# RWKV scan feeding a gated MLP: a group's small matmul runs put side by side

## The chip, the cores and the metric

One core of a Trainium2 chip runs the whole program. The metric is the device time of one launch in microseconds; a kernel's figure is the median of several launches. TensorE (PE in the profile) does the matmuls and writes PSUM, which has eight banks of 512 float32 columns per partition. VectorE (DVE), ScalarE (ACT) and GpSimd (POOL) work beside it, and SyncE (SP) issues nearly all DMAs.

## What is computed

The reference is a linear recurrence over 768 steps for 4 batches and 8 heads of width 48, and then a gated MLP on its output, in float32:

```python
for t in range(S):
    cur = einsum('bhd,bhe->bhde', u * k[t], v[t])
    y[t] = einsum('bhd,bhde->bhe', r[t], state + cur)
    state = w * state + einsum('bhd,bhe->bhde', k[t], v[t])
...
x = y as (3072, 384)
out = (sigmoid(x @ w_gate) * (x @ w_val)) @ w_out     # 384 -> 1536 -> 384
```

## The kernel before

**Attention in groups.** The 768 steps are cut into 12 chunks of 64, and each chunk into two groups of 16 (batch, head) pairs: 24 groups, `n` = 0 to 23. A group needs four runs of 16 small matmuls, all in float32, so the trace counts two passes each and shows 32:

- `from_state` (L314): the decayed state times the queries, into two banks `yb[n]`. It is the first writer of y.
- `scores` (L329): keys times queries, into the two banks `sc`. `keep` (L345) then copies the masked scores to SBUF on VectorE.
- `apply` (L360): masked scores times values, added into the same y banks.
- `outer` (L379): keys times values, the new part of the state, into the upper columns of the y banks. `add_state` (L405) adds it to the state on VectorE, after `decay_state` (L396) on ScalarE.

`x_high` (ScalarE) and `x_low` (VectorE) then split y into two parts for the MLP; `fills` moves some rows of it by DMA. `prepare` makes the next group's inputs on GpSimd and VectorE (`bonus`, `queries`, `keys`, `token_keys`).

**MLP in items.** Two chunks make a tile of 512 columns; there are six tiles (`ti`), with 12 slices of the hidden width (`f`) each. An item is one tile and one slice: `up` (L465, 18 matmuls of 512 columns into two banks), the gate (`sigmoid` on ScalarE, `product` on VectorE, `h_high` on ScalarE, `h_low` on GpSimd), and one item later `down` (L504, 9 matmuls of 512 columns into three accumulators). Weights and activations are split in a high and a low part, which is why there are three passes of everything.

**PSUM.** Eight banks: two for `sc`, three that `one_bank` hands out in turn (`ring`: the two of `up`, and the two of y), three accumulators.

**What sets the order.** The order on all engines is the program's own; each engine works its queue in that order. The first two tiles' groups (0 to 7) and the first tile's items (0 to 13) run in an order written out by hand, the string `START`: there `U.12` is `up` of item 12, `D.11` `down` of item 11, `Z.8` `scores` of group 8, `K` `keep`, `Rv` `queries` on VectorE, `ov` the low part of a weight on VectorE, `A` and `T` `bonus` and `token_keys`. From item 14 on a loop runs: in the slices `SLOTS` (0, 3, 6, 9) of tiles 1 to 4 it takes a group along, for the tile after; that is a slot, and there are 16, groups 8 to 23. TensorE then works `up(i)`, `from_state`, `scores`, `down(i-1)`, `apply`, `outer`, `up(i+1)`. The last tile has items only.

**End of a tile.** `store` (L521) copies the three accumulators, half on ScalarE and half on VectorE, through buffers `wf`, of which the pool has two, and stores them. `store_last` does it for the last tile: accumulators 0 and 1 whole, the third in halves, one on each engine.

Of the kernel before, what the change touches and what calls it, by code (L numbers as in the profile page):

```python
# [19 lines left out]
P = 128  # L20
# [17 lines left out]
SLOTS = (0, 3, 6, 9)  # L38
# [12 lines left out]
W.11 j.9 m.9 I.7 d.7 D.8 ov.8 w.9 o.9 O.7 H.9 h.7 s.7 l.7 F.7 c.10 qv.9 U.10 D.9 g.10 j.10 k.8 w.10  # L51
m.10 U.11 H.10 F.6 c.11 ov.10 g.11 qv.10 D.10 j.11 U.12 m.11 H.11 g.12 qv.11 w.11 A.8 T.8 ov.11 m.12
Rv.8 H.12 D.11 q.12 U.13 g.13 D.12 m.13 H.13 q.13
# [4 lines left out]
def rwkv_then_moe(ctx: ExitStack, tc: tile.TileContext, wd, ch, tk, rt, ut, wt, rk0, vn0, wd0, out):  # L58
# [121 lines left out]
    def token_turn():  # L180
        for be in range(2):
            turn[be] = pacc.tile([P, 512], F32, name=f"acc{be}").rearrange("q (p x) -> q p x", x=64)
        for p in range(NP):
            for a in range(2):
                for be in range(2):
                    row = slice(64 * be, 64 * be + 64)
                    nc.tensor.matmul(
                        turn[be][64 * a : 64 * a + 64, p], pw[row, 2 * p + (a ^ be), 32:96],
                        masks[row, 1], start=True, stop=True,
                    )  # L190
# [58 lines left out]
    xt, dec, ga, yb = {}, {}, {}, {}  # L249
# [26 lines left out]
    def bonus(n):  # L276
        g = GROUPS[n][1]
        r, k = dec_of(n)[:, 1, 0 : 8 * D], toks[n][:, 0, 0 : 8 * D]
        nc.gpsimd.tensor_tensor(r, r, ub[:, g], ALU.mult)
        rows = r.rearrange("q (b p x) -> q b p x", b=2, p=2)  # L280
        nc.gpsimd.tensor_tensor(
            rows, rows, k.rearrange("q (p b x) -> q b p x", b=2, p=2), ALU.mult
        )
        nc.vector.tensor_reduce(
            gains[n % 2], r.rearrange("q (h d) -> q h d", d=D), axis=mybir.AxisListType.X, op=ALU.add
        )
# [73 lines left out]
    def apply(n):  # L360
        c, g = GROUPS[n]
        v, t = toks[n][:, 1], score[n % 2]
        if n < FIRST:
            yb[n] = one_bank(), one_bank()
            if c:
                from_state(n)
                nc.tensor.drain()
        for p, p2 in PP:
            for s in range(2):
                for gm in range(2):  # L370
                    be, row = gm ^ s, slice(64 * gm, 64 * gm + 64)
                    m, at = D if s else 64, (4 * p + 2 * be + p2) * D
                    i = (4 * be + 2 * p + p2) * C
# [5 lines left out]
    def outer(n):  # L379
        k, v = toks[n][:, 0], toks[n][:, 1]  # L380
        for p, p2 in PP:
            for be in range(2):
                for gm in range(2):
                    row, at = slice(64 * gm, 64 * gm + 64), (4 * p + 2 * be + p2) * D
                    m, o = D if be else 64, 256 + (2 * p + p2) * D
                    into_y(
                        n, be, gm ^ be, m, slice(o, o + D), k[row, at : at + m],
                        v[row, at : at + D], True,
                    )
# [15 lines left out]
    def add_state(n):  # L405
        g, st = states(n)
        for s in range(2):
            y = yb[n][s][0:112, 256 : 256 + 4 * D].rearrange("q (p x) -> q p x", p=2)
# [51 lines left out]
    class Moe:  # L460
        def __init__(self, x, acc, cols):
            self.x, self.acc, self.cols = x, acc, cols
            self.pair, self.sg, self.h = {}, {}, {}
# [34 lines left out]
        def gate(self, f):  # L498
# [3 lines left out]
            self.h_low(f)  # L502

        def down(self, f):  # L504

            h, w = self.h.pop(f), (whi[f], wlo[f])
            todo = [(k, d) for k in range(3) for d in range(3)]
            if f == NF - 1:
                todo.sort(key=lambda kd: kd[1])
            for k, d in todo:  # L510
                a, b = PASS[k]
                nc.tensor.matmul(  # L512
                    self.acc[d][:, self.cols], w[a][:, 2 * DM + d * P : 2 * DM + (d + 1) * P],
                    h[:, b, self.cols], start=(f == 0 and k == 0 and self.cols.start == 0),
# [16 lines left out]
    def store_last(acc, c):  # L531
        copies = nc.scalar.copy, nc.vector.tensor_copy
        for d in range(2):
            o = wtmp.tile([P, W3], F32, name="wf")[:, 0:512]
            copies[d](out=o, in_=acc[d])
            nc.sync.dma_start(
                out=out[d * P : (d + 1) * P, c : c + 2], in_=o.rearrange("q (c t) -> q c t", t=CT)
            )
        for i in range(2):
            o = hp.tile([P, 512], F32, name="sg")[:, 0:CT]  # L540
            copies[i](out=o, in_=acc[2][:, i * CT : (i + 1) * CT])  # L541
            nc.sync.dma_start(out=out[2 * P : 3 * P, c + i], in_=o)
# [9 lines left out]
    def moe_of(it):  # L552
# [3 lines left out]
        if (ti, h) not in moes:  # L556
            cols = (slice(0, CT), slice(CT, 2 * CT), slice(0, 2 * CT))[h]
            moes[ti, h] = Moe(xt[ti], accs[ti], cols)
        return moes[ti, h]

    def finish(i):
        ti, h, f = items[i]
        moe_of(items[i]).down(f)
        if f == NF - 1:
            if ti == len(TILES) - 1:
                store_last(accs[ti], TILES[ti][0])
# [6 lines left out]
        "tu": load_gains, "A": lambda n: bonus_keys(n) if n < FIRST else bonus(n), "R": queries,  # L573
# [22 lines left out]

    def prepare(n):
        if n < len(GROUPS):
            bonus(n)
            queries(n)  # L600
            keys(n)
            if GROUPS[n][0] < NC - 1:
                token_keys(n)

    def load(n):
        if n < len(GROUPS):
            load_channels(n)
            load_tokens(n)

    n = FIRST  # L610
    load(n + 1)

    for i in range(n0, len(items)):
# [3 lines left out]
        m.gate(f)  # L617
        attend = f in SLOTS and n < 4 * (ti + 2) and n < len(GROUPS)
        if attend:
            scores(n)  # L620
            if n + 1 < len(GROUPS):
                load_receptance(n + 1)
            if GROUPS[n][0] < NC - 1:
                decay_state(n)
            keep(n)
        finish(i - 1)
        if attend:
            apply(n)
            if GROUPS[n][0] < NC - 1:
                outer(n)  # L630
            x_high(n)
            x_low(n)
            if GROUPS[n][0] < NC - 1:
                add_state(n)
            prepare(n + 1)
            fills(n)
            load(n + 2)
            n += 1
# [193 lines left out]
```

## Time and profile before

| what | value |
|---|---|
| time, median of 3 runs | 562.67 us (561.53 to 564.65) |
| the profiled execution | 565.42 us, of which the span of instructions is 563.5 us |
| mean granted clock of TensorE | 0.982 |
| TensorE busy | 528.8 us (94%) |
| VectorE, GpSimd, ScalarE busy | 221.6, 184.9, 171.3 us |
| HBM | 80 GB/s over the span |

Busy time says which engine to look at. What a stage costs is read from the timeline instead, from one start to the next, since the ends of matmuls are modelled and overlap.

### The profile page before, as it was taken

To read this page: it belongs to the slowest core of one execution; us is meant where nothing else is said; L and a number is where in the kernel's file an instruction comes from. 1 tells how busy PE (TensorE), PEld (TensorE's weight loads), DVE (VectorE), ACT (ScalarE), POOL (GpSimd) and SP (SyncE) were. 2 spreads that over 40 slices of the span, in tenths; PEclk is the share of its full clock that TensorE was granted. 3 is DMA by queue.
4 is the path that set the end of the run, shared out by engine and by line. 5 is a ranking of instruction groups with operands and counts; after the bars stand their busy time and mean duration, and the time that the engine had idled before them with its cause. 6 is when DMAs were issued, how large, how long until landed. Compare 5 with 4: busy or idle time off the path is not lost. (4 is left out here: it accounts for less than half of the span.)

```text
span 563.5 us, 11962 instructions
## 1 busy us (share of the span) xinstructions
PE 528.8 (94%) x5232; PEld 426.7 (76%) x5232; DVE 221.6 (39%) x347; ACT 171.3 (30%) x360; POOL 184.9 (33%) x162
## 2 busy tenths in 40 slices
PE   2587999999899999999999999999999999999995
PEld 2586878787677878778778778788788787888883
DVE  7998988872231331422322412312323321100101
ACT  6564745342121222321221322222322222212211
POOL 3351551404141442433433324424413411211120
PEclk9978999999799999999999999999999999999998
DMA  8895533221400303500203420113220001100001
GB/s 302 331 382 194 228 125 125 33 78 37 168 17 0 92 1 99 192 28 1 91 1 100 132 88 1 50 42 100 94 112 15 11 2 19 58 0 2 0 1 59
DMA packets 15705, 48.02 MB, mean 85 GB/s; under 512 B 2368, under 2 KB 5056, under 8 KB 14240
## 3 DMA queue, kind: packets, MB, share of 16 engines
q1 hardware_dynamic: 15648, 47.20, 24.1%
q8 instruction: 43, 0.70, 0.5%
q14 instruction: 14, 0.11, 0.1%
HBM read 40.12 MB, written 4.72 MB: 80 GB/s over the span
## 5 line engine op out<-in xcount | busy, mean ns | idle before, releaser
L474 PE MATMUL ring<-xt,wx 128*128 128x512 f32 (+1 forms) x1332 | 322.2, 395 | 12.3 <-DVE state L410 5.0
L474 PEld LDWEIGHTS ring<-xt,wx 128*128 128x128 f32 x1332 | 248.0, 192 | 69.8 <-issue 8.6
L496 POOL TENSOR_TENSOR h<-sg,h 128x512 fp32r<-128x512 f32 (+1 forms) x70 | 89.3, 1276 | 336.6 <-ACT h L492 336.6
L512 PE MATMUL acc<-h,wx 128*128 128x512 f32 (+1 forms) x666 | 164.7, 392 | 0.4 <-POOLq L648 0.4
L487 DVE TENSOR_TENSOR sg<-ring,sg 128x512 f32<-128x512 f32 (+1 forms) x74 | 50.0, 676 | 271.5 <-PE ring L474 267.9
L512 PEld LDWEIGHTS acc<-h,wx 128*128 128x128 f32 x666 | 122.1, 189 | 27.9 <-POOLq L648 0.8
L483 ACT ACTIVATE sg<-ring 128x512 f32<-128x512 f32 (+1 forms) x74 | 43.4, 586 | 157.8 <-PE ring L474 157.6
L492 ACT CAST h<-sg 128x512 fp32r<-128x512 f32 (+1 forms) x74 | 45.0, 610 | 152.2 <-DVE sg L487 152.2
L437 DVE TENSOR_TENSOR xt<-ring,xt 112x256 fp32r<-112x256 f32 (+1 forms) x52 | 19.9, 418 | 30.3 <-ACT xt L433 30.2
L433 ACT CAST xt<-ring 112x256 fp32r<-112x256 f32 (+1 forms) x52 | 17.2, 376 | 35.4 <-PE ring L309 31.2
L290 POOL TENSOR_TENSOR dec<-chan,every 128x512 f32<-128x512 f32 x21 | 26.7, 1273 | 0.8 <-DMA chan<-in_ch 0.8
L400 ACT ACTIVATE state<-state,every 112x96 f32<-112x96 f32 x80 | 23.4, 365 | 6.7 <-PE ring L309 6.7
L354 DVE COPY_PREDICATED score<-masks,sc 128x512 f32<-128x512 int32 x32 | 23.9, 747 | 2.0
L300 POOL TENSOR_TENSOR toks<-toks,tabn 128x384 f32<-128x384 f32 x19 | 22.4, 1182 | 4.9 <-PE ring L309 4.9
L309 PEld LDWEIGHTS ring<-score,toks 64*64 64x64 f32 (+1 forms) x768 | 14.5, 136 | 10.5 <-issue 8.2
L236 DVE SCALAR_TENSOR_TENSOR wf<-wr,wf 128x1152 int32<-128x1152 int32 (+1 forms) x13 | 21.5, 1656 | 0.4
L309 PE MATMUL ring<-score,toks 64*64 64x64 f32 (+1 forms) x768 | 17.7, 233 | 3.8 <-DVE score L354 2.4
L246 POOL TENSOR_TENSOR wx<-wf,wx 128x1152 fp32r<-128x1152 f32 (+1 forms) x5 | 12.6, 2528 | 26.2 <-ACT wx L243 26.2
L237 DVE SCALAR_TENSOR_TENSOR wf<-wr,wf 128x1152 int32<-128x1152 int32 (+1 forms) x13 | 20.0, 1541 | 0.5
L296 DVE TENSOR_TENSOR chan<-chan,every 128x512 f32<-128x512 f32 x24 | 19.6, 818 | 1.2 <-ACT dec L272 1.2
L309 PE MATMUL ring<-toks 64*48 64x48 f32 (+1 forms) x704 | 15.5, 220 | 3.4 <-DVE xt L437 3.4
L340 PE MATMUL sc<-dec,chan 48*64 48x64 f32 x768 | 17.1, 229 | 1.2 <-DVE chan L296 1.2
(54 smaller groups left out, 233.3 us busy)
## 6 DMA issues: line engine op xcount, KB each, us to landing
wr<-in_wt SPq DMA_DIRECT2D x11, 1152.0 KB, 7.8
chan<-in_ch SPq DMA_DIRECT2D x24, 512.0 KB, 4.5
toks<-in_tk SPq DMA_DIRECT2D x24, 400.0 KB, 4.5
out_y<-wf SPq DMA_DIRECT2D x17, 256.0 KB, 2.2
dec<-in_rt SPq DMA_DIRECT2D x16, 192.0 KB, 4.1
xt<-xt SPq DMA_DIRECT2D x30, 64.0 KB, 2.3
wr<-in_wt SPq DMA_DIRECT2D x2, 576.0 KB, 6.2
xt<-xt SPq DMA_DIRECT2D x12, 32.0 KB, 4.4
```

Source lines behind the costliest of these rows:

```text
L236: nc.vector.scalar_tensor_tensor(g, high, -(2**31), g, ALU.bitwise_and, ALU.bitwise_or)
L290: eng.tensor_tensor(v4(t[:, 0]), v4(chan[n][:, 0]), bc2(table_of(n)), ALU.mult)
L300: eng.tensor_tensor(v4(k), v4(k), bc2(tabn[:, 4 * g : 4 * g + 4]), ALU.mult)
L309: nc.tensor.matmul(yb[n][bank][64 * half : 64 * half + m, cs], lhsT, rhs, start=first, stop=stop, skip_group_check=True,)
L354: nc.vector.copy_predicated(t.rearrange("q (b m i) -> q b m i", b=2, m=4), masks[:, m].bitcast(I32).unsqueeze(1).unsqueeze(1).broadcast_to ...
L400: nc.scalar.activation(st[:, p, s], st[:, p, s], AF.Copy, scale=pw[0:112, 4 * g + 2 * p + s, 64:65],)
L474: nc.tensor.matmul(o[:, self.cols], w[a][:, g * DM + kt * P : g * DM + (kt + 1) * P], self.x[:, kt, b, self.cols], start=(k == 0), stop=(k ...
L483: nc.scalar.activation(sg[:, c], self.pair[f][0][:, c], AF.Sigmoid)
L487: nc.vector.tensor_tensor(sg[:, c], self.pair.pop(f)[1][:, c], sg[:, c], ALU.mult)
L492: nc.scalar.copy(out=h[:, 0, c], in_=sg[:, c])
L496: eng.tensor_tensor(h[:, 1, c], self.sg.pop(f)[:, c], h[:, 0, c], ALU.subtract)
L512: nc.tensor.matmul(self.acc[d][:, self.cols], w[a][:, 2 * DM + d * P : 2 * DM + (d + 1) * P], h[:, b, self.cols], start=(f == 0 and k == 0 ...
```

## The change

- In a slot the four runs stand together behind `up(i)`: `from_state(n)`, `scores(n+1)`, `outer(n)`, `apply(n)`, and then `down(i-1)`. Scores are thus made one slot ahead; group 8's are made inside `START`, as `Z.8`, with its `Rv.8` and `K.8` and with the preparation of group 9.
- `outer` writes into columns 256 and up of the next group's `sc` banks; `add_state` reads them there.
- Before `apply`, VectorE copies one column of each y bank to a tile `seen`, in place of a drain of TensorE. In the last group and in groups 0 to 7 the drain stands.
- `scores` writes bank `be ^ gm` where it wrote bank `be` (`be` is the half of the rows, `gm` that of the columns); the layouts of the token inputs follow.
- Slots are the slices 1, 4, 7 and 10. `h_high` and `h_low` of a slot's item stand behind the group's work; `prepare` stands an item later, the loads a slot earlier.
- `store` takes both `wf` buffers at once: accumulators 0 and 1 whole in one, the third in the other.
- In the last tile the third accumulator is in two parts of 256 columns in two banks, so `down` has 12 matmuls in place of 9 (6 of 512 and 6 of 256 columns). The last `h_low` is on VectorE. The left part's store is issued by ScalarE.

```diff
-SLOTS = (0, 3, 6, 9)
+SLOTS = (1, 4, 7, 10)
...
-Rv.8 H.12 D.11 q.12 U.13 g.13 D.12 m.13 H.13 q.13
+Rv.8 b.8 Z.8 H.12 D.11 q.12 U.13 g.13 D.12 m.13 K.8 H.13 A.9 R.9 T.9 q.13 k.9
...
-        if n >= FIRST:
-            yb[n] = one_bank(), one_bank()
-            from_state(n)
...
-                        sc[64 * gm : 64 * gm + 64, be, o : o + C],
+                        sc[64 * gm : 64 * gm + 64, be ^ gm, o : o + C],
...
+        yb[n] = one_bank(), one_bank()
+        if c:
+            from_state(n)
+            if n < FIRST or n + 1 == len(GROUPS):
                 nc.tensor.drain()
+            else:
+                scores(n + 1)
+                if GROUPS[n][0] < NC - 1:
+                    outer(n, ga[n + 1][:, :, 256:512])
+                for b in range(2):
+                    nc.vector.tensor_copy(seen[:, b : b + 1], yb[n][b][0:112, 0:1])
...
     def store(acc, dst):
+        two = [wtmp.tile([P, W3], F32, name="wf") for _ in range(2)]
         for d in range(3):
-            o = wtmp.tile([P, W3], F32, name="wf")[:, 0:512]
-            nc.scalar.copy(out=o[:, 0:CT], in_=acc[d][:, 0:CT])
-            nc.vector.tensor_copy(o[:, CT:], acc[d][:, CT:])
+            o = two[d // 2][:, 512 * (d % 2) : 512 * (d % 2) + 512]
+            if d < 2:
+                (nc.scalar.copy, nc.vector.tensor_copy)[d](out=o, in_=acc[d])
+            else:
+                nc.scalar.copy(out=o[:, 0:CT], in_=acc[d][:, 0:CT])
+                nc.vector.tensor_copy(o[:, CT:], acc[d][:, CT:])
...
         m.up(f)
-        m.gate(f)
-        attend = f in SLOTS and n < 4 * (ti + 2) and n < len(GROUPS)
-        if attend:
-            scores(n)
...
-        finish(i - 1)
+        m.sigmoid(f)
+        m.product(f)
+        attend = f in SLOTS and 0 < ti < len(TILES) - 1
...
         if attend:
+            more = GROUPS[n][0] < NC - 1
             apply(n)
-            if GROUPS[n][0] < NC - 1:
-                outer(n)
+            if more:
+                decay_state(n)
             x_high(n)
             x_low(n)
-            if GROUPS[n][0] < NC - 1:
+            if more:
                 add_state(n)
...
+            if n < last:
+                gain(n + 1)
+                keep(n + 1)
...
+        m.h_high(f)
+        m.h_low(f, nc.vector if i == len(items) - 1 else nc.gpsimd)
+        finish(i - 1)
```

Three places show what it moves. In the rows `ring` is a bank of `up` or of y, `sc` the score banks, `acc` an accumulator, `toks` keys and values by token, `dec` the queries, `score` the masked scores.

TensorE in a slot, before: `up`, `from_state`, `scores`, `down`, `apply`, `outer`, `up`.

```order
L474 MATMUL ring<-xt,wx 128x512 x18
L309 MATMUL ring<-dec,state 64x64 x2
...
L340 MATMUL sc<-dec,chan 64x64 x16
L512 MATMUL acc_1633<-h,wx 128x512
...
L309 MATMUL ring<-score_102,toks 64x64 x2
...
L309 MATMUL ring<-toks 64x48 x2
...
L474 MATMUL ring<-xt,wx 128x512 x18
```

The same place in the changed kernel, with what the rows wait for:

```order
L495 MATMUL ring<-xt,wx 128x512 x8
L313 MATMUL ring<-dec,state 64x64 [waits DVE_49]
...
L341 MATMUL sc<-dec,chan 64x64 [waits DMAHW7_49,Pool_49]
L341 MATMUL sc<-dec,chan 64x64 x15
L396 MATMUL sc<-toks 64x48 x2
...
L313 MATMUL ring<-score_102,toks 64x64 [waits DVE_49] x2
...
L533 MATMUL acc_1660<-h,wx 128x512
...
L495 MATMUL ring<-xt,wx 128x512 x9
```

The nine matmuls of `down` no longer stand between the runs, and `apply`, now last, waits for VectorE.

TensorE at the end of `START`, in the changed kernel, from `up` of item 12 to `up` of item 13; before, the row of `sc` was not there:

```order
L495 MATMUL ring<-xt,wx 128x512 x18
L341 MATMUL sc<-dec,chan 64x64 x16
L533 MATMUL acc_433<-h,wx 128x512
L533 MATMUL acc_434<-h,wx 128x512
L533 MATMUL acc_435<-h,wx 128x512
...
L495 MATMUL ring<-xt,wx 128x512 x18
```

And VectorE at that place in the changed kernel: the low part of a weight (`ov.11`), the product of item 12, the queries of group 8, its gains, the product of item 13 and the two copies of `keep`:

```order
L246 TENSOR_TENSOR wx<-wf,wx 128x1152
L508 TENSOR_TENSOR sg<-ring,sg 128x512
L294 TENSOR_TENSOR dec<-chan,every 128x512
L288 TENSOR_REDUCE gain_96<-dec 128x8
L508 TENSOR_TENSOR sg<-ring,sg 128x512
L349 COPY_PREDICATED score_101<-masks,gain_96 128x512
L355 COPY_PREDICATED score_101<-masks,sc 128x512
```

The scores of group 8 now stand on TensorE right behind `up` of item 12, while their queries stand on VectorE behind the product of that same item.

ScalarE where the first tile is stored, before: the decay of the state, the three copies of `store`, the two of `x_high`, the next sigmoid.

```order
L400 ACTIVATE state<-state,every 112x96 x4
L524 COPY wf<-acc_432 128x256
L524 COPY wf<-acc_433 128x256
L524 COPY wf<-acc_434 128x256
L433 CAST xt<-ring 112x2x128 x2
L483 ACTIVATE sg<-ring 128x512
```

And in the changed kernel:

```order
L547 COPY wf<-acc_433 128x512
L549 COPY wf<-acc_435 128x256
L504 ACTIVATE sg<-ring 128x512
L415 ACTIVATE state<-state,every 112x96 x4
L449 CAST xt<-ring 112x2x128 x2
L513 CAST h<-sg 128x512
```

The store's copies stand an item ahead of the slot, and there are two of them.

## Rows read from the trace of the kernel before

**Rows 1.** The page, costliest groups: count, busy us, mean ns, idle before, releaser.

```profile
L474 PE MATMUL ring<-xt,wx 128*128 128x512 f32 (+1 forms) x1332 | 322.2, 395 | 12.3 <-DVE state L410 5.0
```

**Rows 2.** Timeline of TensorE, two plain items: start us, us, what.

```profile
479.69 4.36 PE L474 MATMUL ring<-xt,wx 128*128 128x512 f32 x18
...
485.93 4.35 PE L474 MATMUL ring<-xt,wx 128*128 128x512 f32 x18
```

**Rows 3.** Timeline of TensorE, one slot and the item after it.

```profile
416.65 4.36 PE L474 MATMUL ring<-xt,wx 128*128 128x512 f32 x18
420.94 0.68 PE L309 MATMUL ring<-dec,state 48*64 48x64 f32 x32
421.44 0.65 PE L340 MATMUL sc<-dec,chan 48*64 48x64 f32 x32
...
424.27 0.68 PE L309 MATMUL ring<-score,toks 64*64 64x64 f32 x32
424.77 0.64 PE L309 MATMUL ring<-toks 64*48 64x48 f32 x32
425.34 4.44 PE L474 MATMUL ring<-xt,wx 128*128 128x512 f32 x18
...
431.70 1.55 PE L474 MATMUL ring<-xt,wx 128*128 128x512 f32 x6
```

**Rows 4.** Timeline of TensorE in the hand-written part, runs in a row.

```profile
53.33 1.23 PE L512 MATMUL acc<-h,wx 128*128 128x256 f32 x9
54.49 0.68 PE L309 MATMUL ring<-dec,state 48*64 48x64 f32 x32
55.35 0.68 PE L309 MATMUL ring<-score,toks 64*64 64x64 f32 x32 [0.18 <-issue]
...
57.34 0.96 PE L474 MATMUL ring<-xt,wx 128*128 128x512 f32 x3
```

**Rows 5.** Timeline of VectorE in that slot: the product of its item.

```profile
421.12 0.69 DVE L487 TENSOR_TENSOR sg<-ring,sg 128x512 f32<-128x512 f32 x1 [5.59 <-PE ring L474]
```

**Rows 6.** Groups by shape: the smallest read of PSUM on VectorE.

```profile
L207 DVE TENSOR_REDUCE total<-ring 1x1 f32<-1x8 f32 x1 | 0.2, 153 | 1.4 <-PE ring L206 1.4
```

**Rows 7.** Timeline of TensorE, the first and the third slot that stall.

```profile
139.14 2.36 PE L474 MATMUL ring<-xt,wx 128*128 128x512 f32 x9
144.10 4.18 PE L474 MATMUL ring<-xt,wx 128*128 128x512 f32 x9 [2.60 <-DVE state L410]
...
151.20 1.08 PE L474 MATMUL ring<-xt,wx 128*128 128x512 f32 x4
...
316.54 2.36 PE L474 MATMUL ring<-xt,wx 128*128 128x512 f32 x9
320.06 2.33 PE L474 MATMUL ring<-xt,wx 128*128 128x512 f32 x9 [1.16 <-DVE state L410]
...
324.31 0.86 PE L474 MATMUL ring<-xt,wx 128*128 128x512 f32 x3
```

**Rows 8.** Timeline of ScalarE at the first of these stalls.

```profile
142.21 0.37 ACT L524 COPY wf<-acc 128x256 f32<-128x256 f32 x1 [4.33 <-DMA out_y<-wf]
```

**Rows 9.** Windows: us, busy by engine, granted clock (PEclk), DMA share, GB/s.

```profile
143.50:150.20 6.70, 6.10 (x14) 4.79 (x15) 2.48 (x6) 0.74 (x2) 0.39 (x1) 0.50 0.88 311
```

**Rows 10.** Timeline at the end of `START`: TensorE's `D.11`, and VectorE.

```profile
122.16 2.22 PE L512 MATMUL acc<-h,wx 128*128 128x512 f32 x9
...
122.43 1.36 DVE L246 TENSOR_TENSOR wx<-wf,wx 128x1152 fp32r<-128x1152 f32 x1 [0.39 <-ACT wx L243]
...
124.30 0.68 DVE L290 TENSOR_TENSOR dec<-chan,every 128x512 f32<-128x512 f32 x1
```

**Rows 11.** Timeline of the end of the program.

```profile
554.28 1.28 POOL L496 TENSOR_TENSOR h<-sg,h 128x512 fp32r<-128x512 f32 x1 [4.95 <-ACT h L492]
...
555.62 1.88 PE L512 MATMUL acc<-h,wx 128*128 128x512 f32 x7 [0.36 <-POOLq L648]
...
558.07 0.42 DVE L541 COPY sg<-acc 128x256 f32<-128x256 f32 x1 [0.53 <-ACT sg L541]
```

More of the change, by code (lines that the diff above doesn't have):

```diff
@@ L246, in rest_of_weights @@
         eng.tensor_tensor(wlo[f][:, c], w32[f][:, c], whi[f][:, c], ALU.subtract)
-    xt, dec, ga, yb = {}, {}, {}, {}
+    xt, dec, ga, yb, kv = {}, {}, {}, {}, {}
+    seen = const.tile([112, 2], F32, name="seen")
     PP = [(p, p2) for p in range(2) for p2 in range(2)]
@@ L283, in bonus, with gain @@
         )
+    def gain(n):
+        r = dec_of(n)[:, 1, 0 : 8 * D]
         nc.vector.tensor_reduce(
@@ L377, in apply, with outer @@
                     )
-    def outer(n):
+    def outer(n, banks=None):
         k, v = toks[n][:, 0], toks[n][:, 1]
+        if banks is not None:
+            kv[n] = banks
         for p, p2 in PP:
@@ L460, in rwkv_then_moe, with __init__ @@
     class Moe:
-        def __init__(self, x, acc, cols):
+        def __init__(self, x, acc, cols, last=None):
             self.x, self.acc, self.cols = x, acc, cols
+            c = self.cols
+            self.parts = [(0, acc[0], c, c), (1, acc[1], c, c), (2, acc[2], c, c)]
+            if last is not None:
+                left, right = slice(0, CT), slice(CT, 2 * CT)
+                self.parts[2:] = [(2, acc[2], left, left), (2, last, left, right)]
             self.pair, self.sg, self.h = {}, {}, {}
@@ L501, in gate @@
             self.h_high(f)
-            self.h_low(f)
+            self.h_low(f, eng)
         def down(self, f):
             h, w = self.h.pop(f), (whi[f], wlo[f])
-            todo = [(k, d) for k in range(3) for d in range(3)]
+            todo = [(k, part) for k in range(3) for part in self.parts]
             if f == NF - 1:
-                todo.sort(key=lambda kd: kd[1])
-            for k, d in todo:
+                todo = [(k, part) for part in self.parts for k in range(3)]
+            for k, (d, acc, to, cols) in todo:
                 a, b = PASS[k]
                 nc.tensor.matmul(
-                    self.acc[d][:, self.cols], w[a][:, 2 * DM + d * P : 2 * DM + (d + 1) * P],
-                    h[:, b, self.cols], start=(f == 0 and k == 0 and self.cols.start == 0),
+                    acc[:, to], w[a][:, 2 * DM + d * P : 2 * DM + (d + 1) * P],
+                    h[:, b, cols], start=(f == 0 and k == 0 and self.cols.start == 0),
                     stop=(f == NF - 1 and k == 2),
@@ L528, in store, with store_last @@
             )
-    def store_last(acc, c):
+    def store_last(m, c):
         copies = nc.scalar.copy, nc.vector.tensor_copy
[L533 to L537, printed above, removed]
-            )
[L539 to L542, printed above, removed]
+        for i, (d, acc, to, cols) in enumerate(m.parts):
+            n = to.stop - to.start
+            pool, name = (wtmp, "wf") if d < 2 else (hp, "sg")
+            o = pool.tile([P, W3 if d < 2 else 512], F32, name=name)[:, 0:n]
+            copies[i % 2](out=o, in_=acc[:, to])
+            c0 = c + cols.start // CT
+            (nc.scalar if i == 2 else nc.sync).dma_start(
+                out=out[d * P : (d + 1) * P, c0 : c0 + n // CT],
+                in_=o.rearrange("q (c t) -> q c t", t=CT),
+            )
     halves = [(0, g) for g in range(HALF)] + [(1, g) for g in range(HALF)] + [(2, g) for g in range(HALF, NF)]
@@ L572, in rwkv_then_moe @@
         "L": load_channels, "X": load_tokens, "W": load_weights, "V": load_receptance,
-        "tu": load_gains, "A": lambda n: bonus_keys(n) if n < FIRST else bonus(n), "R": queries,
+        "tu": load_gains, "A": lambda n: bonus_keys(n) if n < FIRST else bonus(n), "b": gain, "R": queries,
         "k": keys, "T": token_keys, "Z": scores, "K": keep, "I": apply, "O": outer,
```

80 lines of the change are left out of this document (42 added, 38 removed).

## The prediction

> **What bounds the kernel now.** I read the page's busy shares first, then the timeline of TensorE from end to end, then the queues of the engines that it waits for. TensorE is busy for 94% of the span, and the page puts most of its idle time ahead of `up` (12.3 us) down to `add_state` [rows 1]. From item 14 on it never waits in a plain item: `up` and `down`, 27 matmuls of 512 columns, take 485.93 - 479.69 = 6.24 us [rows 2]. So time can be won only where TensorE does something else: in slots, in stalls, at the end of `START`, at the end of the program. A stall is read from the bracket behind a row, a slot's price from start to start.
>
> **A slot now.** From `up(i)` to `up(i+1)` it is 425.34 - 416.65 = 8.69 us, and the item after it takes 431.70 - 425.34 = 6.36 [rows 3]. Over two plain items that is 2.45 + 0.12 = 2.57 us for four runs. What do the runs themselves cost? In `START` four runs stand in a row, `apply`, two of `scores` and `outer`: 57.34 - 55.35 = 1.99 us with the way back to big matmuls in it [rows 4]. A run that follows a small one thus takes about 0.47 (the last one 0.57 with the way back, the first 0.50 [rows 3]). Four runs are 1.88, and 2.57 - 1.88 = 0.69 is paid for going from big to small matmuls and back, twice: 0.345 us an excursion.
>
> **The change, part by part.**
>
> *Runs together.* One excursion less in each of 16 slots; `Z.8` in `START` adds one. 15 x 0.345 = **-5.2 us**. On the path in full, since TensorE has no other work there.
>
> *The new wait.* `apply` now waits for the two `seen` copies. On VectorE these stand behind the item's product, which ended at 421.81, 0.87 us after `from_state` began at 420.94 [rows 3, 5]. The nearest row for such a copy is a read of eight columns of PSUM, 0.153 us [rows 6]; two of them end at about 1.18, and with a tenth for the signal TensorE may go at about 1.3. It gets there by itself after three runs, 0.50 + 0.47 + 0.47 = 1.44. So I cost it at nothing: `scores` and `outer` are its cover, with 0.15 us to spare. From below it can't be a gain; from above I take 0.3 us a slot (4.8 us in all), if each copy and signal takes twice as long. What is queued behind `apply` is `down(i-1)` and `up(i+1)`, so any wait is on the path. Group 22 has no `outer`: 0.97 against 1.3, and I put 0.2 there. Group 23 keeps the drain: 55.35 - 54.49 = 0.86 in place of 0.50 [rows 4]. Together **+0.55 us**.
>
> *Score banks.* I cost the new bank of `scores` at nothing: `apply`, which already writes banks `row ^ column`, has the next run 0.50 us after its start, and `from_state`, which writes the bank of its row, has it 0.50 after too [rows 3]. The Trainium skill, page TensorEngine Tiling (Array Packing), section Restrictions and Gotchas, says that different row tiles can't use one PSUM bank at the same time, which speaks against this part. By that rule the scores would take up to twice their 0.47 us, and the sum would be smaller by 7.5 us; the trace's `apply` doesn't show it.
>
> *The four stalls.* In the first slot of each of tiles 1 to 4, `up(i+1)` waits before its second bank, which is a y bank, for `add_state`; four of these waits make the 5.0 us that the page names [rows 1, 7]. The reason is in ScalarE's queue: the third copy of `store` waits 4.33 us for the first store to land, since there are two `wf` buffers, and `x_high` stands behind it [rows 8]. In the changed kernel both buffers are free, `store` is an item ahead of the slot, `add_state` no longer reads the y bank, and between the last run and that bank there are `down(i-1)` and half of `up(i+1)`, some 4.2 us, where there were 2.1. What is late next is `x_low`, two operations on ScalarE and two on VectorE behind `apply`, some 0.4 us each by the copies of the same 256 columns [rows 11]: 1.6 us, hidden. The first stall costs more than its 2.60 us, since TensorE's granted clock behind it is 0.50, its lower level of 1.2 GHz [rows 9]: from 139.14 to 151.20 it is 12.06 us where an undisturbed item after a slot takes 6.36 [rows 3, 7]. That is **-5.7 us**, 2.6 of wait and 3.1 of clock. The third loses 324.31 - 316.54 - 6.36 = 1.41 us for 1.16 of wait [rows 7]; the other two have 5.0 - 2.60 - 1.16 = 1.24 between them, and with the same 0.25 each for starting again 1.74. **-3.15 us**.
>
> *`Z.8` in `START`.* TensorE ends `up` of item 12 at 122.16 and would start the scores of group 8. Their queries come from VectorE, where they stand behind a weight's low part and the product of item 12, and end at 124.30 + 0.68 = 124.98 [rows 10]. Nothing in the change brings these forward (the gains that leave the place ahead of the weight end before it waits for ScalarE). So TensorE stands for 2.8 us, with `D.11` and all that follows behind it: **+2.8 us**. The nearest row for an idle time of this length is the first stall: 2.60 us, and 3.1 us lost to the lower clock [rows 7, 9]. I take that too, **+3.1 us**; from below it is nothing, from above the whole of such a stretch, 6.7 / 2 = 3.35.
>
> *What else moves.* `h_high` and `h_low` of a slot's item now stand behind the runs and `x_high`, and `down(i)` needs them only behind `up(i+1)`, 18 x 0.231 = 4.2 us later than the runs' `down(i-1)`: no cost. `prepare` moves by an item on GpSimd, which is busy for a third of the span, and its results are wanted two items later. On SP the stores come ahead of the slot's loads as before, and loads come a slot earlier. The `fills` of a tile, in its last slot, have `down`, `up` and `down`, 36 x 0.231 = 8.3 us, before the next tile's `up` wants them: 1.6 for `x_low` and a landing of the 4.33 us of rows 8 fit in. `A.9`, `R.9` and `T.9` stand ahead of `q.13` on GpSimd; `D.13` wants it only behind another `up`.
>
> *The end.* The last `h_low` takes 1.28 us on GpSimd, and TensorE stands 0.36 us for it [rows 11]; an operation of that shape on VectorE takes 0.69 [rows 5], so the wait goes: -0.4. The right half of the last accumulator is copied after the left one, 0.53 us of waiting [rows 11]; in two banks the left one goes first, under the right's matmuls: -0.5. Against that, twelve `down`s have six matmuls of 256 columns for three of 512. Nine of these take 54.49 - 53.33 = 1.16 us with a switch in it [rows 4], so 0.118 to 0.129 each, against 6.24 / 27 = 0.231 for 512 columns: 12 x (6 x 0.118 - 3 x 0.231) = 0.2 us, at most 1.0. Together **-0.7 us**.
>
> **The sum.** -5.2 + 0.55 - 5.7 - 3.15 + 2.8 + 3.1 - 0.7 = -8.3 us. It is made against the profiled execution, 565.4 us (its span is 563.5), and gives 557.1 there. The median of before is 2.75 us lower, its runs 3.1 us apart, about the size of the one loss of clock. Since the change takes one such loss away and puts a like one in, I carry the difference over: 562.67 - 8.3 = **554.4 us**.
>
> **The rivals.**
>
> *The clock stays up behind `Z.8`.* The stall is not longer than some that had no such price (1.16 us at 320.06 lost only 0.25 more [rows 7]), and it might be cut by a queue that I read too late. Then 3.1 us less: 551.3. Chance 0.15.
>
> *`apply` waits a little.* For it: the margin is 0.15 us, worked out from a row of another shape. Against it: the product's end is the same in every slot. At 0.3 us a slot it is 554.4 + 4.8 = 559.2. Chance 0.12.
>
> *Scores run at half speed in shared banks.* 16 x 0.47 = 7.5 us: 561.9. Against it stands `apply`'s run [rows 3]. It is the page's rule named above. Chance 0.03.
>
> *Slower than before: the `seen` copies come only when all three runs are done.* If VectorE hears of `from_state` only with the last of the small matmuls, some 0.2 us after the third run (a run lasts 0.65 us, the next begins after 0.5 [rows 3]), then two copies and a signal, 0.4, follow, and TensorE stands for 0.6 us in 15 slots: 9.0 us, 563.4. The point from which this turns the sign is 8.3 / 15 = 0.55 us a slot. Against it: the product of an item starts 0.18 us after `from_state` has begun [rows 3, 5], so VectorE hears of one group's end with others already behind it. Chance 0.04.
>
> That the change doesn't do what it says can be left out: the order of the instructions shows the runs together.
>
> **How the numbers follow.** The forecast has a chance of 0.63, the rivals 0.15, 0.12, 0.03 and 0.04, and 0.03 are left for what I don't see, mostly small. The predicted time is that of the forecast. The range reaches down to the clock that stays up with half a microsecond to spare, 550.8, and up to the waiting `apply`, 559.2: it leaves out about 0.1 and the unsure size of the other terms. Half a percent, about what a measurement of this kernel can tell from no change, is 2.8 us: faster means below 559.9. The forecast and the first two rivals are there, less a little for the edge of the second: 0.87. The last two rivals are within half a percent, and with that edge make 0.10. Slower keeps 0.03, for what I don't see.
>
> **What would show it.** Right: slots of 8.35 us from `up` to `up` with no bracket behind any row of `apply`; no bracket on `up` named after `state`; one bracket of 2.5 to 2.9 us at the scores behind `up` of item 12, released by `dec`, and a stretch at 1.2 GHz after it; none in the last `down`. Wrong: brackets at `apply` released by `seen`; a score run longer than 0.5 us; `down` of the last tile over 2.2 us; a new stall at the first `up` of a tile, released by a DMA.

## The result, and the profile after

| what | before | after |
|---|---|---|
| time, median | 563.66 us (561.53 to 565.01, 4 runs) | 555.27 us (553.81 to 555.54, 4 runs) |
| ratio, with its 95% interval | | 0.985 (0.981 to 0.989) |
| profiled execution, and its span | 565.42 us, 563.5 us | 555.54 us, 553.8 us |
| mean granted clock | 0.982 | 0.992 |

The changed kernel is faster by 1.5%, 8.4 us between the medians. The forecast was 554.4 us, the range 550.8 to 559.2. The two profiled spans are 9.8 us apart.

The page of the changed kernel first: the span, the engines, and the groups of `up` and `scores`.

```profile
span 553.8 us, 12047 instructions
...
PE 522.1 (94%) x5268; PEld 428.6 (77%) x5268; DVE 226.1 (41%) x373; ACT 171.5 (31%) x355; POOL 184.1 (33%) x161
...
L495 PE MATMUL ring<-xt,wx 128*128 128x512 f32 (+1 forms) x1332 | 319.3, 394 | 6.3 <-issue 3.9
...
L341 PE MATMUL sc<-dec,chan 48*64 48x64 f32 x768 | 17.7, 231 | 5.0 <-DVE dec L294 2.7
```

TensorE is still busy for 94%, of a shorter span. The idle time ahead of `up` is 6.3 us where it was 12.3, and `state` is no longer its first releaser [rows 1]. The scores have a new one of 2.7 us, released by `dec`.

A slot and the item after it, in the timeline of TensorE, which answers to [rows 3]:

```profile
414.70 4.36 PE L495 MATMUL ring<-xt,wx 128*128 128x512 f32 x18
418.99 0.68 PE L313 MATMUL ring<-dec,state 48*64 48x64 f32 x32
419.49 0.65 PE L341 MATMUL sc<-dec,chan 48*64 48x64 f32 x32
419.96 0.58 PE L396 MATMUL sc<-toks 64*48 64x48 f32 x30
420.33 0.25 PE L313 MATMUL ring<-score,toks 64*48 64x64 f32 x2
420.37 0.23 PE L396 MATMUL sc<-toks 64*64 64x48 f32 x2
420.42 0.66 PE L313 MATMUL ring<-score,toks 64*48 64x64 f32 x30
421.00 2.32 PE L533 MATMUL acc<-h,wx 128*128 128x512 f32 x9
423.17 4.35 PE L495 MATMUL ring<-xt,wx 128*128 128x512 f32 x18
...
429.41 1.79 PE L495 MATMUL ring<-xt,wx 128*128 128x512 f32 x7
```

Four runs stand in a row and take 421.00 - 418.99 = 2.01 us. No row has a bracket. From `up` to `up` it is 423.17 - 414.70 = 8.47 us, and the next item takes 429.41 - 423.17 = 6.24; before, 8.69 and 6.36. `apply` starts 420.33 - 418.99 = 1.34 us after `from_state`. What it waits for stands in VectorE's timeline, which answers to [rows 5]:

```profile
419.17 0.69 DVE L508 TENSOR_TENSOR sg<-ring,sg 128x512 f32<-128x512 f32 x1 [5.56 <-PE ring L495]
419.78 0.21 DVE L374 COPY seen<-ring 112x1 f32<-112x1 f32 x2
```

The two `seen` copies end at 419.99, 1.00 us after `from_state` began, with 0.34 us to spare. In group 22, which has no `outer`, they end at 440.94, and `apply` starts at 440.94 too, 0.99 us after its `from_state`: there nothing is to spare.

The first slot of the second tile, the place of the first stall in [rows 7, 8]: TensorE, then ScalarE's copy of the third accumulator.

```profile
150.43 4.35 PE L495 MATMUL ring<-xt,wx 128*128 128x512 f32 x18
...
156.68 3.66 PE L495 MATMUL ring<-xt,wx 128*128 128x512 f32 x15
...
142.17 0.37 ACT L549 COPY wf<-acc 128x256 f32<-128x256 f32 x1 [0.15 <-PE acc L533]
```

`up` runs through in 6.25 us, and the copy waits for TensorE, not for a store. The same holds in the other three tiles.

The end of `START`, TensorE first and then VectorE, answers to [rows 10]; the last row is a window as in [rows 9].

```profile
119.61 4.36 PE L495 MATMUL ring<-xt,wx 128*128 128x512 f32 x18
126.71 0.69 PE L341 MATMUL sc<-dec,chan 48*64 48x64 f32 x32 [2.73 <-DVE dec L294]
127.33 2.31 PE L533 MATMUL acc<-h,wx 128*128 128x512 f32 x9
129.48 4.36 PE L495 MATMUL ring<-xt,wx 128*128 128x512 f32 x18
...
124.09 1.36 DVE L246 TENSOR_TENSOR wx<-wf,wx 128x1152 fp32r<-128x1152 f32 x1 [0.84 <-ACT wx L243]
125.37 0.68 DVE L508 TENSOR_TENSOR sg<-ring,sg 128x512 f32<-128x512 f32 x1
125.97 0.68 DVE L294 TENSOR_TENSOR dec<-chan,every 128x512 f32<-128x512 f32 x1
...
127.50:131.00 3.50, 3.50 (x16) 2.88 (x17) 0.00 (x0) 0.00 (x0) 3.42 (x4) 1.00 0.03 7
```

The stall came where the prediction put it, 2.73 us long, with the weight, the product and the queries ahead on VectorE. But the granted clock behind it is 1.00 in this execution.

And the end of the program, for [rows 11]: VectorE, TensorE, the two last copies, SyncE's last store.

```profile
545.25 0.69 DVE L517 TENSOR_TENSOR h<-sg,h 128x512 fp32r<-128x512 f32 x1 [0.69 <-ACT h L513]
...
545.71 1.90 PE L533 MATMUL acc<-h,wx 128*128 128x512 f32 x9
...
547.70 0.37 ACT L562 COPY sg<-acc 128x256 f32<-128x256 f32 x1 [0.50 <-PE acc L533]
548.00 0.42 DVE L562 COPY sg<-sc 128x256 f32<-128x256 f32 x1
...
548.94 0.42 SPq L564 DMA_DIRECT2D out_y<-sg  x1
```

The wait for GpSimd's `h_low` is gone. The last copy ends at 548.42, but its store is issued half a microsecond later, since SyncE is busy with another one.

### The profile page after: what moved, and what is told of

Read it like the earlier page. It is cut to its first block, busy times and chain, and to the rows that moved or that the text cites. A ratio compares the mean times of both kernels' runs of the same rounds, so it can differ in the third digit from the quotient of the medians.

```text
span 553.8 us, 12047 instructions
## 1 busy us (share of the span) xinstructions
PE 522.1 (94%) x5268; PEld 428.6 (77%) x5268; DVE 226.1 (41%) x373; ACT 171.5 (31%) x355; POOL 184.1 (33%) x161
## 4 chain that ended last, share of the span: by engine, by line
PE 76%; DVE 0%; issue 0%
PE ring L495 46%; PE acc L533 23%; PE ring L313 3%; PE sc L341 1%; PE sc L396 1%; PE sc L533 1%; DVE wf L562 0%; DVE dec L294 0%; DVE sg L562 0%; PE ring L206 0%
## 5 line engine op out<-in xcount | busy, mean ns | idle before, releaser
L533 PE MATMUL acc<-h,wx 128*128 128x512 f32 (+1 forms) x666 | 161.6, 383 | 0.0
L533 PEld LDWEIGHTS acc<-h,wx 128*128 128x128 f32 x666 | 119.6, 188 | 24.4
L341 PEld LDWEIGHTS sc<-dec,chan 48*64 48x64 f32 x768 | 15.1, 145 | 6.5 <-DVE dec L294 3.2
L313 PEld LDWEIGHTS ring<-score,toks 64*48 64x48 f32 (+1 forms) x768 | 15.3, 133 | 5.1 <-issue 4.6
L313 PEld LDWEIGHTS ring<-dec,state 48*48 48x48 f32 (+1 forms) x704 | 12.4, 130 | 7.5 <-issue 6.5
```

What stands on the lines that cost most here:

```text
L313: nc.tensor.matmul(yb[n][bank][64 * half : 64 * half + m, cs], lhsT, rhs, start=first, stop=stop, skip_group_check=True,)
L341: nc.tensor.matmul(sc[64 * gm : 64 * gm + 64, be ^ gm, o : o + C], kk[row, cs : cs + C], rr[row, cs : cs + C], start=True, stop=True,)
L533: nc.tensor.matmul(acc[:, to], w[a][:, 2 * DM + d * P : 2 * DM + (d + 1) * P], h[:, b, cols], start=(f == 0 and k == 0 and self.cols.start ...
```

## The experiments

Each ratio is to runs of the kernel before taken beside the experiment, whose median lay between 563.9 and 565.4 us; microseconds of different experiments are comparable only to that extent.

**Scores of group 8 one `up` later.** Only the place of `Z.8` in `START` differs from the changed kernel.

```diff
-Rv.8 b.8 Z.8 H.12 D.11 q.12 U.13 g.13 D.12 m.13 K.8 H.13 A.9 R.9 T.9 q.13 k.9
+Rv.8 b.8 H.12 D.11 q.12 U.13 Z.8 g.13 D.12 m.13 K.8 H.13 A.9 R.9 T.9 q.13 k.9
```

> The changed kernel with Z.8 (the scores of group 8) moved in START from behind up of item 12 to behind up of item 13. Theory (the stall there is only the place: queries that VectorE ends 2.7 us after up of item 12): the bracket of 2.73 us at the first score row goes, no new one comes, and the program is 2.7 us shorter than the changed kernel: span 551.1 against 553.8, about 552.7 us. Rival (the time is given back, since VectorE is behind in START and up of item 13 or a later step waits for it): the bracket comes back under another row, over 1.5 us, and the time stays at 554.5 to 556.

Measured: 551.37 us (551.03 to 553.39, 6 runs), ratio to before 0.976 (0.973 to 0.980), span 551.3 us. Timeline of TensorE from `up` of item 13:

```profile
126.30 4.36 PE L495 MATMUL ring<-xt,wx 128*128 128x512 f32 x18
130.59 0.69 PE L341 MATMUL sc<-dec,chan 48*64 48x64 f32 x32
```

The stall is gone and nothing comes in its place: from `up` of item 12 to `up` of item 14 it is 13.32 us, in the changed kernel 16.11. The median is 3.9 us below that of the changed kernel, more than the 2.8 us of this place; the rest isn't traced. With the last version below, which is built on it, this is the fastest of the kernels that were run.

**The kernel before with the new store alone.**

```diff
     def store(acc, dst):
+        two = [wtmp.tile([P, W3], F32, name="wf") for _ in range(2)]
         for d in range(3):
-            o = wtmp.tile([P, W3], F32, name="wf")[:, 0:512]
-            nc.scalar.copy(out=o[:, 0:CT], in_=acc[d][:, 0:CT])
-            nc.vector.tensor_copy(o[:, CT:], acc[d][:, CT:])
+            o = two[d // 2][:, 512 * (d % 2) : 512 * (d % 2) + 512]
+            if d < 2:
+                (nc.scalar.copy, nc.vector.tensor_copy)[d](out=o, in_=acc[d])
+            else:
+                nc.scalar.copy(out=o[:, 0:CT], in_=acc[d][:, 0:CT])
+                nc.vector.tensor_copy(o[:, CT:], acc[d][:, CT:])
```

> The kernel before with the new store alone (both wf buffers taken at once, accumulators 0 and 1 copied whole); slots, runs and y banks as before. Theory (the four stalls are the third copy's wait for the first store to land): no bracket on up named after state any more, the lower clock behind the first stall gone with it, 8.9 us less: 554.5 to 556 in the median. Rival (the slot's place and add_state's read of the y bank make the stalls): brackets stay, at least 0.5 us in each of the four slots, and the time stays above 560.

Measured: 556.49 us (556.22 to 556.61), ratio 0.985 (0.981 to 0.989), span 554.4. The place of the first stall on TensorE, with the slots still at 0, 3, 6 and 9 and the runs apart:

```profile
138.76 4.44 PE L474 MATMUL ring<-xt,wx 128*128 128x512 f32 x18
...
145.13 4.34 PE L474 MATMUL ring<-xt,wx 128*128 128x512 f32 x18
```

No bracket, 6.37 us for the item. Over tiles 1 to 4, from `up` to `up` twelve items later, the gains are 5.69, 0.88, 1.39 and 0.84 us. The whole stall was the store's wait for a landing, as the prediction read it out of [rows 8]. The ratio, 0.985, is that of the whole change too: what the runs win by standing together, the changed kernel loses again at `Z.8` and elsewhere in `START`.

**The changed kernel with the old store.** The diff above, the other way round.

> The changed kernel with the old store (three wf buffers in turn out of two, every copy in halves). Theory (the wait for the first store to land is then in ScalarE's queue ahead of the next item's sigmoid, and the slot is that next item): from_state's second bank or apply waits for it in the first slot of tiles 1 to 4, a bracket of 0.4 to 1.5 us each, 2 to 6 us in all: 557 to 561. Rival (moving the slots an item on and outer into the score banks is enough, the buffers are not needed): no such bracket, 554.5 to 556.

Measured: 556.04 us (555.12 to 556.55), ratio 0.984 (0.979 to 0.988), span 554.7. ScalarE ahead of a first slot (that of `ti` = 2), TensorE behind `Z.8`, and the clock there:

```profile
229.30 0.37 ACT L545 COPY wf<-acc 128x256 f32<-128x256 f32 x1 [2.35 <-DMA out_y<-wf]
...
126.42 3.89 PE L533 MATMUL acc<-h,wx 128*128 128x512 f32 x9
...
126.90:130.20 3.30, 3.30 (x10) 2.56 (x9) 0.00 (x0) 0.00 (x0) 3.22 (x4) 0.50 0.03 7
```

ScalarE waits for the landing as before, but an item ahead of the slot, and TensorE doesn't wait for it: from item 14 on every item takes as long as in the changed kernel, to 0.03 us. So with the new slots the new store gains nothing. And here the clock did fall behind `Z.8`: `down` takes 3.89 us where it took 2.31.

**Old store and old slots, the rest changed.** In addition to the old store:

```diff
-SLOTS = (1, 4, 7, 10)
+SLOTS = (0, 3, 6, 9)
```

> The changed kernel with the old store and with the slots back at slices 0, 3, 6 and 9, so that a tile's first slot is again the item in which the tile before is stored. Theory (the wait for the first store only hurts because the store's copies stand ahead of x_high in ScalarE's queue, and a y bank is wanted half an up later; in the new order of the runs the copies stand behind x_high, and the bank is wanted 4.2 us later): no bracket on up in any slot, ScalarE still waits 2 to 4 us for a store to land, span 553 to 555 if the clock stays up behind Z.8. Rival (it is the slot's place, an item behind the store, that removed the stalls): brackets of 0.5 us and more on up in the first slots of tiles 1 to 4, span above 556.

Measured: 559.32 us in one run, span 557.4. The item behind a first slot, TensorE, VectorE and SyncE's stores:

```profile
149.58 1.88 PE L533 MATMUL acc<-h,wx 128*128 128x512 f32 x7 [0.47 <-DVE wf L546]
...
149.10 0.42 DVE L546 COPY wf<-acc 128x256 f32<-128x256 f32 x1 [2.26 <-ACT wf L545]
...
146.54 3.35 SPq L547 DMA_DIRECT2D out_y<-wf  x3
```

Neither theory is right as it stands. `up` no longer waits. `add_state` reads another bank, and `x_high`, `x_low` and `add_state` stand ahead of the store's copies; which of the two does it, this run doesn't show. But the third accumulator is copied late. VectorE's half of the first copy stands behind the slot's work, so the first store leaves at 146.54 us only; it lands after 2.06 us, and ScalarE's third copy starts at 148.70, right behind that landing. Now `down` of the next item waits for it: 7.02 us in place of 6.25, four times, 3.1 us.

**Old slots, new store.** Only the line of `SLOTS` differs from the changed kernel.

> The changed kernel with slots at the slices 0, 3, 6 and 9 again, the new store kept. With the old store this move cost 0.77 us in each of four slots, at the third accumulator of the item behind the slot, whose copy stood behind a store that had to land. Theory: that wait was the old store's alone; with both buffers taken at once nothing waits for a landing, so no row of down in an item behind a first slot has a bracket, the item takes 6.25 us, and the span is that of the changed kernel, 553.8 us (553.3 to 555.6, the upper end if the clock falls behind Z.8). Rival: the slot at slice 0 itself is the cause, since the copies of the old tile then stand on ScalarE and VectorE behind x_high, x_low and add_state and end too late for down of the next item; then a bracket of 0.3 to 0.8 us on down, released by a wf copy, in four items, and a span of 555 to 557.

Measured: 555.68 us (554.77 to 555.92), ratio 0.984 (0.981 to 0.988), span 552.7. The same place as in the run above:

```profile
142.45 4.35 PE L495 MATMUL ring<-xt,wx 128*128 128x512 f32 x18
146.64 2.22 PE L533 MATMUL acc<-h,wx 128*128 128x512 f32 x9
148.69 3.66 PE L495 MATMUL ring<-xt,wx 128*128 128x512 f32 x15
```

No bracket, 6.24 us: the theory holds. VectorE's copies are late here too, as the rival has it (the last one ends at 145.27 us), but no landing stands behind them, and `down` doesn't wait. Its span lies 1.0 us below the changed kernel's because `START` was 1.8 us shorter and the end 0.7 longer, of which more below. In the changed kernel the new store and the new slots thus each take the stall away alone; together they gain it once.

**Two excursions again.** `apply` behind `down(i-1)`, the other three runs as changed.

```diff
...
+            finish(i - 1)
+            add_values(n)
             x_high(n)
...
-        finish(i - 1)
+        if not attend:
+            finish(i - 1)
```

> The changed kernel with apply of groups 8 to 23 moved behind down(i-1), so that a slot has two excursions to small matmuls again: from_state, scores, outer, then down, then apply; all else as in the changed kernel. Theory (an excursion costs 0.35 us whatever runs are in it): slots 0.35 us longer, 16 x 0.35 = 5.6 us more than the changed kernel: span 559.4, about 561 us. Rival (the gain of the slots comes from the scores made a slot ahead and from the freed y banks, not from the order of the runs): under 1.5 us more, 555 to 557.

Measured: 561.27 us (559.74 to 562.45, 10 runs), ratio 0.994 (0.991 to 0.996), span 559.4. The slot on TensorE:

```profile
227.36 4.36 PE L500 MATMUL ring<-xt,wx 128*128 128x512 f32 x18
...
235.44 0.68 PE L313 MATMUL ring<-score,toks 64*64 64x64 f32 x32
236.05 4.44 PE L500 MATMUL ring<-xt,wx 128*128 128x512 f32 x18
```

The slot takes 8.69 us again and the next item 6.37. An excursion has its price wherever it stands, and the span is the theory's.

**The drain in place of `seen`.**

```diff
-                for b in range(2):
-                    nc.vector.tensor_copy(seen[:, b : b + 1], yb[n][b][0:112, 0:1])
+                nc.tensor.drain()
```

> The changed kernel with a drain of TensorE ahead of apply in every slot, in place of the two seen copies. Theory (a drain costs what it costs in the last group, where the step from from_state to the next run is 0.86 us in place of 0.50): 0.36 us in 15 slots, 5.4 us more: span 559, about 560.5 us; the copies are worth as much as putting the runs together. Rival (behind two more runs the drain finds the array nearly empty of what it waits for): under 0.1 us a slot, 555 to 557.

Measured: 560.94 us (560.24 to 561.58), ratio 0.993 (0.990 to 0.996), span 559.8. From `outer` to `apply` on TensorE:

```profile
233.52 0.64 PE L395 MATMUL sc<-toks 64*48 64x48 f32 x32
234.28 0.68 PE L313 MATMUL ring<-score,toks 64*64 64x64 f32 x32
```

0.76 us where the changed kernel has 420.33 - 419.96 = 0.37. A slot and the two items behind it take 0.33 us longer than in the changed kernel, 5.0 us in 15 slots. Without `seen` nearly the whole gain of putting the runs together is lost. (The expectation took its 0.86 us from `START`; in the last group of the changed kernel the step with the drain is 0.81.)

**The last tile not in halves.** The old `store_last`; the last `h_low` stays on VectorE.

```diff
...
-            last = two_banks()[:, 0] if ti == len(TILES) - 1 else None
-            moes[ti, h] = Moe(xt[ti], accs[ti], cols, last)
+            moes[ti, h] = Moe(xt[ti], accs[ti], cols)
```

> The changed kernel with the last tile as before: nine matmuls in each down, the third accumulator whole, its halves copied one after the other, all stores from SP; the last h_low stays on VectorE. Theory (the halves win 0.5 us at the end and cost 0.2 to 0.4 us in twelve downs): items of the last tile 6.25 us in place of 6.28, the stretch from the last up to the end 0.5 to 0.9 us longer, span within 0.5 us of 553.8 if the clock does the same. Rival (the halves make the end, and the downs cost nothing): span 0.8 us longer.

Measured: 558.62 us in one run, span 556.8. Items of the last tile take 6.25 us, in the changed kernel 6.28; eleven of them give 0.35 us back. From the last `up` to the end it is 14.68 us, in the changed kernel 14.33. By these two profiles the halves are worth nothing. The 3.0 us of its longer span are the clock, which fell behind `Z.8` here too (1.65), and `START` (1.36), where TensorE stands for 1.07 us inside a run of scores:

```profile
70.19 0.45 PE L341 MATMUL sc<-chan,dec 48*64 48x64 f32 x12 [1.07 <-issue]
```

**The changed kernel once more.**

> The changed kernel unchanged, one more profile, for two things that differ between kernels in which nothing at that place differs. First the clock behind the idle time at Z.8 (2.7 us in every one of them): it stayed at 1.00 in four profiles and fell to 0.50 for some 3.4 us in two. If the fall is set by the kernel, this profile has 1.00 again and up of item 12 to up of item 13 takes 9.87 us; if it is a matter of the execution, it may be 0.50, 11.5 us and a span longer by 1.6. A second 1.00 leaves it open. Second the gap of 1.09 us inside the scores at 35.5 us, which no engine or semaphore explains: it came in five of six kernels that contain the change, 0.54 to 1.09 us long, and in neither of the two without it. If it belongs to the changed program it is here again after seven passes, by 0.5 to 1.1 us; if it is chance, it may be absent.

Measured: 556.21 us, span 554.3. The window behind `Z.8`, and the scores at 35 us on TensorE:

```profile
127.50:130.60 3.10, 3.10 (x9) 2.43 (x8) 0.00 (x0) 0.00 (x0) 3.02 (x4) 0.50 0.00 0
...
35.21 0.58 PE L341 MATMUL sc<-dec,chan 48*64 48x64 f32 x25 [1.23 <-issue]
```

The same program, and this time the clock fell. From `up` of item 12 to `up` of item 14 it is 17.77 us, 16.11 in the first profile: the fall costs 1.66 us. The gap inside the scores is there again. The expectation counted it in five of six kernels; all seven profiles of the change that lay before it have the gap, the shortest 0.37 us.

**The right half's store on ScalarE,** on top of the version with the scores later.

```diff
-            (nc.scalar if i == 2 else nc.sync).dma_start(
+            (nc.scalar if i >= 2 else nc.sync).dma_start(
```

> The version with the scores of group 8 behind up of item 13, and the store of the right half of the last accumulator issued by ScalarE, like the left one's, where SyncE issued it. In the changed kernel the right half was copied by 548.42 us, but SyncE, busy with the store of accumulators 0 and 1, issued its store at 548.94 only; ScalarE is free at 548.48. Theory: the last store to be issued sets the end, so it moves ahead by some 0.45 us less what the issue on ScalarE takes longer: from up of the last item to the end 13.8 us in place of 14.2, span 550.9 (551.3 without this edit, give or take what the start of the program takes). Rival: what ends last is the landing of accumulator 1's store, still issued by SyncE until 548.8, or what the program does after it; then 14.2 us as before.

Measured: 551.85 us (550.34 to 552.86), ratio 0.978 (0.972 to 0.983), span 550.7. The last issues, and the landings of all stores:

```profile
544.41 1.01 ACTq L564 DMA_DIRECT2D out_y<-sg  x2
...
DMA to landing us min/median/max: 2.0/2.3/4.2
```

From the last `up` to the end it took 15.02 us; the theory said 13.8, the rival 14.2. Both missed. The issue did move ahead, from 9.63 to 9.16 us behind that `up`, but the store then took 4.20 us to land, where it took 2.79 without the edit. In eleven of the twelve profiles the span ends 1.65 to 1.80 us behind the last landing of a store (2.86 with the drain), so a landing is what comes last; why this one took longer is open. In all twelve profiles this stretch is 15.1 us with the last `h_low` on GpSimd (two) and 14.2 to 15.0 with it on VectorE (ten): it differs by more than the issue can win. No gain that can be told.

## Why the prediction was right, and where it was not

The terms against the two profiled spans, 563.55 and 553.76 us:

| term | forecast | measured | from |
|---|---|---|---|
| excursions and the new wait | -4.65 | -4.88 | groups 9 to 23 -5.44, group 8 -0.34, `Z.8`'s run beyond its idle time +0.90 |
| the first stall | -5.7 | -5.70 | `up` of 13 to `up` of 16: 26.99 to 20.95, less the slot's 0.34 |
| the other three | -3.15 | -3.11 | the store alone: 0.88, 1.39, 0.84 |
| `Z.8` waits for its queries | +2.8 | +2.73 | the bracket |
| the clock behind it | +3.1 | 0 | window at 1.00 |
| `START` up to `up` of item 12 | 0 | +1.64 | 117.97 to 119.61 |
| the last tile and the end | -0.7 | -0.47 | 83.86 to 83.39 |
| sum | -8.3 | -9.79 | spans: -9.8 |

**Runs together: right.** With the store's effect taken out (the kernel before with the new store against the changed one) a tile of four slots gained 1.44 us, 0.36 a slot, where 0.345 was worked out of [rows 3, 4]. Moving `apply` back took the same away, 0.37 a slot. The sign that was named, 8.35 us from `up` to `up`, didn't come, since a third of the gain lies in the item behind the slot: 8.47 for 8.69, and 6.24 for 6.36.

**The new wait: right.** Forecast were an end of the copies at 1.18 us and `apply` at 1.44; it is 1.00 and 1.34. `outer` and `apply` overlap a little, which the price of 0.47 a run didn't have. The tenth for the signal isn't seen either: in group 22, where 0.2 us of waiting were forecast, `apply` starts at the end of the copies, 0.99 us after `from_state`, where 1.3 was forecast.

**Score banks: right.** The scores take 419.96 - 419.49 = 0.47 us, the price of a run out of [rows 4]. The Trainium skill (TensorEngine Tiling (Array Packing), Restrictions and Gotchas) says that different row tiles can't use one PSUM bank at the same time. The rival that reads this as a price in time, 7.5 us in all, isn't borne out by this row.

**The stalls: right in size, and one of two reasons too many.** The store's wait was the cause, as the first experiment on the old kernel shows. The prediction put the new buffers, the item of distance and the other bank side by side. The buffers do it alone, in the kernel before as in the changed one with old slots. The distance does it too, at least together with the other bank and the new order on ScalarE and VectorE. The other bank and that order, without the distance and the buffers, only move the wait from `up` to `down`, at 0.77 us each.

**The clock behind `Z.8`: the step that failed.** "I take that too" carried 3.1 us over from the first stall, [rows 9], on the length of the idle time alone. In eight profiles with this stall, 2.73 to 2.79 us long in all, the clock fell in three and stayed in five. Where it fell it stayed low for some 3.4 us, half as long as in [rows 9], and cost 1.6 to 1.7 us. So the term is between 0 and 1.7, and the forecast's 3.1 lay above the whole of it. The profiled execution is the rival with a chance of 0.15; its argument was off, though, since the stall of 1.16 us that it points to is shorter than this one. The version with the scores later confirms the rest: without the idle time there is no fall.

**`START`: a term that was missing.** Nothing of the change was thought to cost there, apart from `Z.8`. Two things did. On TensorE, the second part of the scores at 35 us and the first `up` behind 47 us, in the changed kernel:

```profile
35.55 0.58 PE L341 MATMUL sc<-dec,chan 48*64 48x64 f32 x25 [1.09 <-issue]
...
48.11 7.03 PE L495 MATMUL ring<-xt,wx 128*128 128x256 f32 x36 [3.89 <-issue]
```

The same two in the kernel before:

```profile
34.83 0.64 PE L340 MATMUL sc<-dec,chan 48*64 48x64 f32 x29
...
47.47 6.02 PE L474 MATMUL ring<-xt,wx 128*128 128x256 f32 x36 [3.89 <-issue]
```

TensorE stops inside a run of scores, and no semaphore makes it wait. The bracket is in all ten profiles that hold the change, 0.37 to 1.40 us, at the same instruction, and in neither of the two without it; but with the new store alone TensorE takes a step of 0.19 us there too, too short for a bracket. The traces hold a likely reason, which no experiment tested. It lies in a DMA queue of the page:

```profile
q8 instruction: 43, 0.70, 0.5%
```

One of its packets, of 16 KB, ends at 33.2 to 34.7 us in each of the twelve profiles, and the score behind the gap starts 1.34 to 1.59 us after that end in all of them. In the two without the change it does so as well, 1.51 and 1.45 us after, but there TensorE comes to that score only then, or 0.2 us before. Three more such gaps, each at one instruction, stand 1.26 to 1.62 us behind such a packet too: at 25 us in several profiles, the kernel before among them, at 41 us in others, and at 70 us, as with the last tile not in halves. So TensorE seems to wait for its instructions. Why their packet comes later, or TensorE earlier, in the changed kernel is open. The second is the clock: behind 2.5 to 3.9 us of idle time it is low for 6.8 us in some profiles and for 3.4 in others. The changed kernel had one of each, 7.03 and 6.03 us for the same 36 matmuls. This 1.0 us is the execution's, not the change's.

**The end: right direction, too much.** GpSimd's 0.36 us went. What the halves win in copies the six matmuls of 256 columns give back, and the landing of the last stores blurs the rest.

**The carry to the median.** The forecast lowered the median of before by the sum, since its profiled run lay 2.75 us above it. The changed kernel's profiled run lies only 0.27 above its own median. So for the profiled execution the sum asked for 557.1 us, 1.6 more than it took, while the forecast of the median is 0.9 too low: the missing `START`, the clock's 3.1 and this carry partly cancel, and that the hit is closer than its steps is luck.

## What to carry to other kernels

Price a run of small matmuls by what it costs to go to it and back, here 0.35 us, and put such runs side by side; look for a signal from another engine in place of a drain, if work of TensorE's own covers it. Work that is moved ahead in the program must be followed to the producer of what it waits for: one `up` more between `Z.8` and its queries was worth 2.8 us at its place. If a stall can be removed by a free buffer or by distance, one of the two is enough; here the buffer alone, in the kernel before, gave the whole ratio of the change.

## What the runs showed of the hardware

The clock does not fall behind every idle time of TensorE of one length: of eight like ones of 2.7 to 2.8 us three were followed by a stretch at 1.2 GHz, and the same program did both. What such a stretch costs when it comes, 1.6 to 1.7 us here, is a price to be weighed with a chance.

The landing of a store took 2.0 to 4.4 us in these profiles, 2.1 to 2.5 in the median of each. A wait like the 4.33 us of [rows 8] is one of the long ones: the same copy waited 2.34 us in the changed kernel with the old store, and the copies at the other three stalls of the kernel before 2.32 to 2.88 us.
